# A planner that holds matmuls of another array form back for a while, in a fused attention and two-layer-pair kernel on one core

## The chip, the core and the metric

The kernel runs on one core of a Trainium2 chip. Its engines work side by side, each from its own queue in order: TensorE (PE for matmuls, PEld for the weight loads that precede them), VectorE (DVE), ScalarE (ACT), GpSimd (POOL) and SyncE (SP, which issues nearly all DMAs here). The metric is the device time of one execution in microseconds. Before the change it was 1039.26 us, the median of three runs (1038.78 to 1040.11).

## The reference

Three blocks follow one another. The attention has 4 batches of 8 heads, 576 tokens and 64 columns a head; `f` gives a decay that is added to the scores. Both feed-forward blocks take 2304 tokens of 512 columns through 2048 inner columns.

```
scores = q @ k.T / sqrt(D) + (cum[:, None] - cum[None, :])     # cum = cumsum(log f)
scores = where(causal, -1e9, scores)
attn   = softmax(scores);  x = attn @ v                        # (B, H, S, D) -> (B*S, H*D)
h = x @ w1_in;  g = h * sigmoid(1.702 * h);        x = g @ w1_out
h = x @ w2_in;  g = max(h, 0) + alpha * min(h, 0); out = g @ w2_out
```

All is float32, so most operands are split into a high and a low half, and each product is three matmuls (high by high, high by low, low by high).

## The kernel before

**No hand-written order.** The kernel first describes its work as some thousands of operations (`plan.add`), each with the engines that it may run on, a modelled duration, what it reads and writes, a priority `pri` (a small number goes first) and, for matmuls, a `mode`. Then `Plan.run` (L106) plays all engines through at once: it looks at every operation whose inputs are planned, works out when each could start, takes the one that could start earliest, and among equals the one with the smallest `pri`. What it takes is fixed on its engine at that moment. The list, sorted by planned start, is the program. On the chip every engine goes through its own list in order and waits where something is late; nothing is rearranged there.

**Mode.** TensorE's array can be used in three forms here. Mode 0 is the whole array (128 rows by 128 columns): the turns of q and k (L561), the turn of the maxima (L692), the score products of the last 64 queries (L659, L660), the products of weights and values with split halves (L755), and all products of the feed-forward blocks (L863 for x @ w1_in). Mode 1 uses two halves of 64 rows, one head in each: scores for the maxima (L666), scores for the exponentials (L791), and the product for the 64-row key tile (L732 with a 64-column output). Mode 2 uses two halves of 64 columns (L726, the values of the first 256 queries). The planner adds `SWITCH` = 105 to a matmul operation's modelled end when its mode differs from the one before it (L138); the choice of the next operation (L143, L144) does not look at mode.

**Attention.** Heads go in pairs, queries of a pair in two chunks: 0 to 256 and 256 to 576. That makes 32 chunks; batch 0 has its eight first (four small, four large), then batches 1 to 3 alternate small and large: 12 pairs. A chunk goes through scores for the maximum (L666, L659), masked maximum on DVE (L675), a turn of the maxima (L692) and its eviction (L702), scores again with the maximum as a term (L791), exponentials on ACT (L798), masking on POOL (L714). From chunk 8 on, large chunks split the weights into halves `eh` (a copy on ACT, L370) and `el` (a difference on DVE or POOL, L375), and L755 multiplies `eh` and then `el` by the values. Then DVE normalises (L815 to L832) into the ring `xr`. Two chunks are in work at once.

**Filler.** x @ w1_in (`gemm1`, L842) has seven blocks of 256 or 384 tokens, 16 times 12 matmuls each, 1344 in all. A block may start when the attention has finished its tokens. Its `pri` is 1000 and more, the attention's is 100 to 140, so it fills TensorE wherever no attention operation can start. Its operands `xh` (ACT) and `xl` (DVE) have three and two buffers, so the next block's are made while the last one ends. After the attention, w1_out is converted on ACT and DVE (L501 to L509, L370, L375) while the rest of the filler runs; then come the other three products (L952, L1042, L1120), all in mode 0.

Of the kernel before, what the change touches and what calls it, by code (L numbers as in the profile page):

```python
# [20 lines left out]
BD = 300  # L21
WLAG = 2500.0
SWITCH = 105.0
QUEUE = {"SP": "SP", "ACTQ": "ACT"}


# [46 lines left out]
class Plan:  # L73
# [32 lines left out]
    def run(self):  # L106
        free = {}
        dma = 0.0
        mode = 0
        avail = [o for o in self.ops if o.nd == 0]  # L110
        out = []
        while avail:
            best = None
            for o in avail:
                t0 = o.ready
                need = {}
                for b in o.bufs:
                    t0 = max(t0, b.begin)
                    if b.pool is not None and b.slot is None:
                        p = b.pool  # L120
                        r = p.ready()
                        i = need[p] = need.get(p, -1) + 1
                        if p.nxt + i != b.idx or len(p.free) <= i or p.nxt + i - p.gone >= p.n or r is None:
                            t0 = None
                            break
                        t0 = max(t0, r, p.free[i][0])
                if t0 is None:
                    continue
                alt = None
                for eng, dur, *more in o.alts:  # L130
                    bias, port = (*more, 0.0, False)[:2] if len(more) < 2 else more
                    t = max(t0, free.get(QUEUE.get(eng, eng), 0.0))
                    if port:
                        t = max(t, free.get("port", 0.0))
                    if eng in QUEUE:
                        end = max(t + 1500.0, dma) + dur + 750.0
                    else:
                        end = t + dur + (SWITCH if eng == "PE" and o.mode != mode else 0.0)  # L138
                    key = end + bias
                    if alt is None or key < alt[0]:  # L140
                        alt = (key, t, eng, end, port)
                _, t, eng, end, port = alt
                if best is None or (t, o.pri, end, o.seq) < best[0]:  # L143
                    best = ((t, o.pri, end, o.seq), o, eng, port)  # L144
            assert best is not None, "no operation can start"
            (t, _, end, _), o, eng, port = best
            avail.remove(o)
            o.start, o.eng = t, eng
            if eng == "PE":
                mode = o.mode  # L150
            if eng in QUEUE:
                free[QUEUE[eng]] = t + 480.0
                dma = end - 750.0
            else:
                free[eng] = end
                if port:
                    free["port"] = end
            for b in o.bufs:
                if b.pool is not None and b.slot is None:
                    b.begin, b.slot = b.pool.free.pop(0)  # L160
                    b.begin = max(b.begin, b.pool.ready())
                    b.pool.nxt += 1
            for b in o.bufs:
                b.left -= 1
                b.end = max(b.end, end + LAT)
                if b.left == 0 and b.pool is not None:
                    p = b.pool
                    p.gone += 1
                    p.end = max(p.end, b.end)
                    p.free.append((b.end, b.slot))  # L170
                    p.free.sort()
            for s in o.succ:
                lat = 0.0 if (eng == "PE" and all(a[0] == "PE" for a in s.alts)) else LAT
                s.ready = max(s.ready, end + lat + o.lag)
                s.nd -= 1
                if s.nd == 0:
                    avail.append(s)
            out.append(o)
        assert len(out) == len(self.ops)
        out.sort(key=lambda o: (o.start, o.seq))  # L180
        for o in out:
            o.fn(o.eng)
        return max(o.start for o in out)
# [988 lines left out]
```

## Time and profile before

| | |
|---|---|
| median of the runs | 1039.26 us |
| profiled execution | 1043.87 us, its span 1042.0 us |
| PE / PEld busy | 1012.6 us (97%) / 882.3 us (85%) |
| DVE / ACT / POOL busy | 724.6 (70%) / 514.3 (49%) / 118.1 us (11%) |
| chain that ended last | PE 82%, DMA 7%, DVE 4%, ACT 3%, issue 2% |
| mean granted clock of TensorE | 0.989 of full speed |

The profile shows one execution. "Busy" adds up what an engine's instructions cover; a matmul's end is modelled, and matmuls overlap, so two matmuls' distance from start to start says more about the pace than the duration of one. The chain of waits is followed back from the last instruction to what released it. A row of the timeline joins equal instructions that follow one another; x2 is two of them. Of the two matmuls in a row of L666 or L791, one runs in each half of the array.

### The profile page before, as it was taken

The numbers are of one execution on the slowest core, as the hardware profiler recorded it, in microseconds if no ns is written. First come the engines' busy times: TensorE is split into PE (matmuls) and PEld (weight loads), VectorE is DVE, ScalarE is ACT, GpSimd is POOL, SyncE is SP. The second block draws the span as 40 slices with busy tenths as digits, with TensorE's granted clock in tenths as the row PEclk, the third lists the DMA queues.
The fourth block names the chain that finished last, engine by engine and source line by source line (L and its number), as shares of the span: only waits on it lengthen the run. The fifth ranks groups of instructions, "written<-read, shape, count | busy, mean of one in ns | idle before, by whom it ended". The sixth has DMA issues, their size and how long they took to land.

```text
span 1042.0 us, 17821 instructions
## 1 busy us (share of the span) xinstructions
PE 1012.6 (97%) x6187; PEld 882.3 (85%) x6187; DVE 724.6 (70%) x1528; ACT 514.3 (49%) x1071; POOL 118.1 (11%) x203
## 2 busy tenths in 40 slices
PE   7799999999999999999999999999999999999997
PEld 4477788888888899998888898999999988888886
DVE  5688887777766692109998565676994876676773
ACT  4367654453444483228776464455863742222322
POOL 5133422211221000000000000000300110000000
PEclk8899999999999999999999999999999999999999
DMA  4577744323311195225667354465775443443441
GB/s 104 120 195 185 186 111 89 73 66 76 76 52 44 47 295 179 102 92 163 220 193 228 100 148 141 166 196 167 221 268 176 156 128 115 118 142 84 126 140 65
DMA packets 180089, 144.69 MB, mean 139 GB/s; under 512 B 101152, under 2 KB 155088, under 8 KB 180000
## 3 DMA queue, kind: packets, MB, share of 16 engines
q1 hardware_dynamic: 180000, 143.57, 47.0%
q8 instruction: 48, 0.79, 0.3%
q14 instruction: 41, 0.34, 0.1%
HBM read 96.14 MB, written 47.33 MB: 138 GB/s over the span
## 4 chain that ended last, share of the span: by engine, by line
PE 82%; DMA 7%; DVE 4%; ACT 3%; issue 2%; SPq 1%; POOL 1%; ACTq 0%; DVEq 0%; POOLq 0%
PE bk L1120 19%; PE bk L863 17%; PE bk L952 17%; PE bk L1042 11%; PE bk L791 5%; PE bk L755 4%; DMA wraw<-in_moe_w_out_dram 3%; PE bk L726 3%; PE bk L666 2%; PE bk L732 2%; DMA h2scr<-go 1%; DMA wraw<-in_moe_w_in_dram 1%; DMA rk<-in_k_dram 1%; PE bk L659 1%; DVE wraw L506 1%
## 5 line engine op out<-in xcount | busy, mean ns | idle before, releaser
L863 PE MATMUL bk<-xh,wA 128*128 128x384 f32 (+1 forms) x896 | 224.1, 321 | 0.0
L370 ACT CAST qh<-qg 128x512 fp32r<-128x512 f32 (+1 forms) x159 | 91.9, 579 | 171.6 <-DVE qg L918 118.0
L375 DVE TENSOR_TENSOR ql<-qg,qh 128x512 fp32r<-128x512 f32 (+1 forms) x158 | 100.5, 637 | 101.4 <-PE bk L952 49.5
L863 PEld LDWEIGHTS bk<-xh,wA 128*128 128x128 f32 x896 | 158.6, 190 | 12.2 <-issue 8.5
L1120 PE MATMUL bk<-wS,qh 128*128 128x512 f32 x576 | 145.7, 389 | 0.0
L863 PE MATMUL bk<-xl,wA 128*128 128x384 f32 (+1 forms) x448 | 140.7, 314 | 0.6 <-DVE xl L375 0.6
L1120 PEld LDWEIGHTS bk<-wS,qh 128*128 128x128 f32 x576 | 108.1, 188 | 22.4
L1042 PE MATMUL bk<-xsb,wS 128*128 128x384 f32 x576 | 108.9, 336 | 3.2 <-DVE go L1064 2.7
L370 ACT COPY gg<-bk 128x384 f32<-128x384 f32 (+1 forms) x112 | 48.7, 435 | 122.1 <-PE bk L863 119.3
L1042 PEld LDWEIGHTS bk<-xsb,wS 128*128 128x128 f32 x576 | 100.2, 188 | 6.0 <-DVE go L1064 4.4
L675 DVE CUSTOM_DVE_ANT_0 bk<-bk,mask 128x512 f32<-128x512 f32 (+4 forms) x160 | 75.3, 496 | 38.6 <-PE bk L666 35.3
L952 PE MATMUL bk<-qh,woa 128*128 128x512 f32 (+1 forms) x440 | 99.5, 368 | 0.1
L952 PEld LDWEIGHTS bk<-qh,woa 128*128 128x128 f32 x440 | 77.3, 189 | 14.2 <-ACT qh L370 0.5
L863 PEld LDWEIGHTS bk<-xl,wA 128*128 128x128 f32 x448 | 85.2, 190 | 1.2 <-DVE xl L375 1.0
L798 ACT ACTIVATE e<-bk 128x384 f32<-128x384 f32 (+3 forms) x192 | 59.5, 400 | 51.0 <-PE bk L791 46.0
L1042 PE MATMUL bk<-xsa,wS 128*128 128x384 f32 x432 | 82.5, 334 | 0.0
L1120 PE MATMUL bk<-wS,ql 128*128 128x512 f32 x288 | 80.4, 389 | 0.0
L1042 PEld LDWEIGHTS bk<-xsa,wS 128*128 128x128 f32 x432 | 75.6, 188 | 0.2
L911 DVE SCALAR_TENSOR_TENSOR qg<-qg,qr 128x512 f32<-128x512 f32 (+1 forms) x80 | 50.8, 636 | 24.6 <-ACT qg L910 24.4
L1120 PEld LDWEIGHTS bk<-wS,ql 128*128 128x128 f32 x288 | 54.0, 188 | 11.2
L910 ACT ACTIVATE qg<-qr 128x512 f32<-128x512 f32 (+1 forms) x80 | 46.9, 588 | 22.0 <-DVE ql L375 18.9
L952 PE MATMUL bk<-ql,woa 128*128 128x512 f32 (+1 forms) x220 | 54.1, 368 | 0.0
(161 smaller groups left out, 1748.0 us busy)
## 6 DMA issues: line engine op xcount, KB each, us to landing
h2scr<-go SPq DMA_DIRECT2D x96, 192.0 KB
wraw<-in_moe_w_in_dram SPq DMA_DIRECT2D x32, 512.0 KB
wraw<-in_moe_w_out_dram SPq DMA_DIRECT2D x32, 512.0 KB
qr<-h1scr SPq DMA_DIRECT2D x64, 256.0 KB
qr<-h2scr SPq DMA_DIRECT2D x64, 256.0 KB
h1scr<-gg SPq DMA_DIRECT2D x64, 192.0 KB
ba<-y1scr SPq DMA_DIRECT2D x24, 384.0 KB
h1scr<-gg SPq DMA_DIRECT2D x48, 128.0 KB
```

The source lines that it names most:

```text
L370: nc.scalar.copy(dst, src)
L375: E[e].tensor_tensor(dst, a, b, op=ALU.subtract)
L675: plan.add([("DVE", c_dve(c1 - c0) + 90.0)], lambda e, pm=pm, c0=c0, c1=c1, mk=mk, m0=m0, col=col, f0=f0: nc.vector.tensor_tensor_reduce(p ...
L755: nc.tensor.matmul(pb[hh].ap[:l.shape[1], s0 - q0:n], l, rhs.ap[:w, hh, :m], start=st, stop=sp, skip_group_check=True,)
L791: nc.tensor.matmul(pss[hh].ap[:w, o_:o_ + m], x.ap[r, a:a + w], y.ap[r, s0 - q0:n], start=i == 0, stop=i == 3, skip_group_check=True)
L798: plan.add([("ACT", c_act(x1 - x0, True))], lambda e, hh=hh, pss=pss, e32=e32, w=w, x0=x0, x1=x1: nc.scalar.activation(e32.ap[:w, hh, :x1 ...
L863: nc.tensor.matmul(ph.ap[:, :n], w.ap[:, a, c, :], x[c // 2].ap[:, c % 2, :n], start=(c == 0 and j == 0), stop=(c == KT - 1 and j == 2))
L910: plan.add([("ACT", c_act(n))], lambda e: nc.scalar.activation(g.ap[:, :n], raw.ap[:, :n], AF.Tanh, scale=0.851), [raw], [g], pri)
L911: plan.add([("DVE", c_dve(n), 0.0, True)], lambda e: nc.vector.scalar_tensor_tensor(g.ap[:, :n], g.ap[:, :n], 1.0, raw.ap[:, :n], op0=ALU. ...
L952: nc.tensor.matmul(py[d].ap[:, :n], w[:, a, d * P:(d + 1) * P], (lo if x else h).ap[:, :n], start=(k == 0 and (a, x) == (0, 0)), stop=(k = ...
L1042: nc.tensor.matmul(out.ap[:, :XH], w[:, a, t, c, :], x.ap[:, b, c, :], start=(st and c == 0 and i == 0), stop=(c == 1 and i == 2), skip_gr ...
L1120: nc.tensor.matmul(py[t].ap, (lo if x else h).ap[:, t * P:(t + 1) * P], w[:, a], start=(k == 0 and (a, x) == (0, 0)), stop=(k == NM - 1 an ...
```

## The change

Two constants are added, and the planner's choice is altered. A TensorE operation whose mode is not the current one, and whose inputs and buffers have been there for less than 2000 ns of planned time, is ranked as if it started 250 ns later; its planned start, once it is taken, stays the true one. So as long as an operation of the current form can start within 250 ns, it goes first, whatever the priorities; after 2000 ns the rank is the old one. Nothing is computed in another way: the program has the same 4173 rows of TensorE instructions, in another order.

```
+PEN = 250.0
+HOLD = 2000.0
...
                 _, t, eng, end, port = alt
-                if best is None or (t, o.pri, end, o.seq) < best[0]:
-                    best = ((t, o.pri, end, o.seq), o, eng, port)
+                hold = PEN if eng == "PE" and o.mode != mode and t - t0 < HOLD else 0.0
+                if best is None or (t + hold, o.pri, end, o.seq) < best[0]:
+                    best = ((t + hold, o.pri, end, o.seq), o, eng, port, t)
             assert best is not None, "no operation can start"
-            (t, _, end, _), o, eng, port = best
+            (_, _, end, _), o, eng, port, t = best
```

Because of the added lines, a line from L150 on has a number that is 3 higher in the changed kernel (L863 is L866 there).

**TensorE, a middle pair of chunks.** Names: `bk` is a PSUM bank, `KH`, `QH`, `QL`, `KL` are halves of k and q, `DK`, `DQ` hold decay and maximum, `eh`, `el` halves of the weights, `VH`, `VL`, `VR` the values, `xh`, `xl`, `wA` operands of the filler. Before, scores of a new small chunk stand between products with values, and the first maximum scores of a large chunk follow alone, with filler behind them:

```order
L791 MATMUL bk_88<-DQ_100,DK_95 128x256
L791 MATMUL bk_84<-DQ_100,DK_95 128x256
L755 MATMUL bk_86<-eh_1600,VH_107 128x320
L755 MATMUL bk_81<-eh_1600,VH_107 128x320
L755 MATMUL bk_86<-eh_1600,VL_109 64x320
L755 MATMUL bk_81<-eh_1600,VL_109 128x320
L755 MATMUL bk_86<-el_1630,VH_107 128x320
L755 MATMUL bk_81<-el_1630,VH_107 128x320
L666 MATMUL bk_85<-KH_174,QH_258 128x384
L666 MATMUL bk_83<-KH_174,QH_258 128x384
L666 MATMUL bk_85<-DK_95,ones 128x384
L666 MATMUL bk_83<-DK_95,ones 128x384
```

With the change, the maximum scores of the large chunk, the waiting 64-row product (L735) and the small chunk's scores stand in one run:

```order
L669 MATMUL bk_86<-KH_230,QH_233 128x384
L669 MATMUL bk_82<-KH_230,QH_233 128x384
L669 MATMUL bk_86<-DK_96,ones 128x384
L669 MATMUL bk_82<-DK_96,ones 128x384
L735 MATMUL bk_88<-e_377,VR_104 128x64
L735 MATMUL bk_85<-e_377,VR_104 128x64
L794 MATMUL bk_84<-QH_177,KH_230 128x128
L794 MATMUL bk_81<-QH_177,KH_230 128x128
L794 MATMUL bk_84<-QL_184,KH_230 128x128
L794 MATMUL bk_81<-QL_184,KH_230 128x128
L794 MATMUL bk_84<-QH_177,KL_236 128x128
L794 MATMUL bk_81<-QH_177,KL_236 128x128
```

The twelve rows before hold two changes of form (at the first L755 and the first L666), and filler follows as a third; the twelve rows after hold none. Counted by form over the whole program, with L726 as a form of its own, there are 232 changes before and 153 after. Up to the 224th matmul of L791, which ends the first eight chunks, it is 50 and 42; behind it, 182 and 111. A middle pair of chunks goes from 16 to 18 changes to 8.

**DVE, the `el` halves of the same kind of chunk.** Before, the first two `el` of a large chunk follow two copies of the next q and k and stand together:

```order
L372 CAST QH_233<-tq_837 128x256
L372 CAST KH_230<-tk_856 128x576
L375 TENSOR_TENSOR el_1630<-e_456,eh_1600 128x640
L375 TENSOR_TENSOR el_1619<-e_384,eh_1594 128x640
L375 TENSOR_TENSOR QL_240<-tq_837,QH_233 128x256
L375 TENSOR_TENSOR KL_236<-tk_856,KH_230 128x576
L540 STREAM_TRANSPOSE tq_837<-rq_130 128x320
```

With the change, a small chunk's normalisation (reciprocal, L825, L835) and a q half stand around and between them:

```order
L824 RECIPROCAL rc_399<-sm_392 128x8
L378 TENSOR_TENSOR el_1556<-e_532,eh_1533 128x640
L825 STREAM_TRANSPOSE tr_385<-rc_399 128x256
L378 TENSOR_TENSOR QL_240<-tq_789,QH_233 128x256
L835 TENSOR_TENSOR xr<-bk_83,tr_385 128x256
L378 TENSOR_TENSOR el_1540<-e_377,eh_1523 128x640
```

What stands ahead of the second `el` behind the first is now three instructions more.

**ACT, the end of the attention.** `wc`, `wraw` are weights being converted, `qh` an operand of L952, `gg` an evicted filler product. Before, the copies `xh` of a filler block come late in the conversion of w1_out:

```order
L501 ACTIVATE wc_518<-wraw_405 128x512
L370 COPY gg_722<-bk_84 128x384
L502 ACTIVATE wraw_405<-wraw_405 128x512
L501 ACTIVATE wc_499<-wraw_412 128x512
L370 COPY gg_815<-bk_88 128x384
L502 ACTIVATE wraw_412<-wraw_412 128x512
L370 COPY gg_680<-bk_83 128x384
L370 CAST xh_1095<-xr 128x768
L370 COPY gg_722<-bk_82 128x384
L370 CAST xh_473<-xr 128x768
```

With the change they stand in the middle of it, since the filler is further on:

```order
L504 ACTIVATE wc_515<-wraw_425 128x512
L373 CAST qh_4630<-qg_4561 128x512
L505 ACTIVATE wraw_425<-wraw_425 128x512
L373 CAST qh_4642<-qg_4537 128x512
L373 COPY gg_694<-bk_87 128x384
L373 CAST woa_4655<-wc_554 128x512
L373 CAST xh_1100<-xr 128x768
L373 COPY gg_787<-bk_88 128x384
L373 CAST xh_490<-xr 128x768
```

When the attention's last product is issued, 750 filler matmuls have been issued before and 852 after. From there to the first L952 it is 210 of them before and 108 after; from that L952 on, TensorE's order is the same in both.

## Rows read from the trace of the kernel before

**Rows 1.** Six stretches, TensorE first: busy us and instructions per engine, clock, DMA share, GB/s.

```profile
0.00:107.00 107.00, 89.24 (x661) 66.31 (x662) 77.13 (x221) 59.42 (x145) 38.36 (x82) 0.92 0.63 152
107.00:358.00 251.00, 248.75 (x2100) 209.05 (x2099) 188.54 (x528) 115.89 (x306) 57.01 (x106) 0.99 0.34 81
358.00:465.00 107.00, 106.37 (x610) 105.51 (x610) 38.91 (x66) 48.96 (x95) 0.00 (x0) 1.00 0.49 164
465.00:660.00 195.00, 194.88 (x951) 164.97 (x950) 150.96 (x268) 126.84 (x226) 0.00 (x0) 1.00 0.53 164
660.00:838.00 178.00, 174.76 (x995) 171.92 (x994) 132.81 (x207) 107.74 (x205) 16.75 (x11) 1.00 0.61 200
838.00:1042.00 204.00, 198.62 (x880) 164.52 (x878) 136.28 (x240) 55.45 (x97) 5.98 (x4) 0.99 0.38 112
```

**Rows 2.** What TensorE waited for: us in total, times, longest us.

```profile
PE bk L666 <- DMA DK<-xr: 4.9, 2, 4.4
PE bk L1042 <- DVE go L1064: 2.7, 3, 1.3
PE bk L666 <- ACT e L798: 2.2, 1, 2.2
```

**Rows 3.** Timeline of TensorE in a middle pair: start us, us, instruction.

```profile
228.08 0.31 PE L791 MATMUL bk<-DQ,DK 64*128 64x320 f32 x2
...
229.13 0.39 PE L863 MATMUL bk<-xh,wA 128*128 128x256 f32 x1
...
230.04 0.41 PE L791 MATMUL bk<-QH,KH 64*128 64x320 f32 x2
230.28 0.31 PE L791 MATMUL bk<-QL,KH 64*128 64x320 f32 x2
...
230.58 0.31 PE L791 MATMUL bk<-DQ,DK 64*128 64x320 f32 x2
230.82 0.34 PE L692 MATMUL bk<-ident_r,MX 128*67 128x128 f32 x2
...
233.03 0.56 PE L755 MATMUL bk<-el,VH 128*128 128x320 f32 x2
...
238.49 0.41 PE L863 MATMUL bk<-xh,wA 128*128 128x256 f32 x2
...
238.84 0.40 PE L863 MATMUL bk<-xh,wA 128*128 128x256 f32 x2
...
244.49 0.66 PE L726 MATMUL bk<-e,VR 128*64 128x128 f32 x8
```

**Rows 4.** The same pair on ScalarE, timeline.

```profile
228.42 2.05 ACT L798 ACTIVATE e<-bk 128x320 f32<-128x320 f32 x8 [1.30 <-PE bk L791]
230.34 1.37 ACT L370 CAST eh<-e 128x640 fp32r<-128x640 f32 x2
```

**Rows 5.** The same pair on VectorE, timeline.

```profile
231.37 1.55 DVE L375 TENSOR_TENSOR el<-e,eh 128x640 fp32r<-128x640 f32 x2
```

**Rows 6.** ScalarE behind the attention, timeline.

```profile
362.86 1.14 ACT L370 CAST woa<-wc 128x512 fp32r<-128x512 f32 x2
...
377.49 0.63 ACT L370 CAST woa<-wc 128x512 fp32r<-128x512 f32 x1
```

**Rows 7.** VectorE at the end of a filler block, timeline.

```profile
396.64 1.82 DVE L375 TENSOR_TENSOR xl<-xr,xh 128x768 fp32r<-128x768 f32 x2
```

**Rows 8.** TensorE at the same place, timeline.

```profile
394.83 2.01 PE L952 MATMUL bk<-qh,woa 128*128 128x512 f32 x8
...
397.65 0.45 PE L863 MATMUL bk<-xl,wA 128*128 128x384 f32 x1 [0.63 <-DVE xl L375]
```

**Rows 9.** SyncE near the start, timeline of DMA issues.

```profile
32.62 5.19 SPq L612 DMA_DIRECT2D VR<-in_v_dram  x2
```

**Rows 10.** TensorE near the start, timeline.

```profile
41.18 0.69 PE L666 MATMUL bk<-DK,ones 64*128 64x384 f32 x2 [4.37 <-DMA DK<-xr]
```

**Rows 11.** A short stretch by itself, columns as in rows 1.

```profile
118.00:122.00 4.00, 4.00 (x20) 2.64 (x20) 3.70 (x11) 1.24 (x5) 2.43 (x3) 0.57 0.69 215
```

## The prediction

> **What bounds the kernel now.** I read the stretches first, then what TensorE waited for, then the timeline of one pair of chunks on three engines. In the stretch from 107 to 358 us, where the attention of batches 1 to 3 runs among the filler, matmuls cover 248.75 of 251 us; to 107 us they cover only 89.24, and behind 358 us nearly everything [rows 1]. The waits of TensorE are few: 4.9 us for the DMA of the decay near the start, 2.2 us for exponentials, 2.7 us in the third product [rows 2]. ACT and DVE have 115.89 and 188.54 busy us in the 251 us of the middle stretch [rows 1], so TensorE's own work is what sets the time there, and whatever is taken out of its list comes out of the end, unless something else becomes late.
>
> Busy is not the same as fast, though, and the timeline shows where. Steady filler of 256 columns goes from start to start in (238.84 - 238.49) / 3 = 0.117 us. A lone run of six, between two runs of 64-row scores, takes from 229.13 to 230.04, 0.91 us, where six steady ones take 0.70: 0.21 us too much. A lone run of eight 64-row score matmuls takes from 230.04 to 230.82, 0.78 us, where four steady pairs of 0.15 us (230.28 to 230.58 for two) take 0.60: 0.18 us too much [rows 3]. Each run pays once, so a change of form costs between 0.18 and 0.21 us. I take 0.19.
>
> The Trainium skill ("Trainium Kernel Development and Optimization", Performance Expectations) says that busy time of matmuls is a poor measure of how near TensorE is to its limit and that the busy share of weight loads is a better one. By matmul time the middle stretch has 2.25 us to give; by weight loads it would have 251 - 209.05 = 42 us, which the sum below does not use.
>
> **The change part by part.** *Changes of form.* From the order there are 232 before and 153 after. The first eight chunks account for 50 and 42, what follows for 182 and 111. The 71 that go in the later part are in the stretch where TensorE does not wait [rows 1]: 71 x 0.19 = 13.5 us. By the two ends of the cost it is 71 x 0.18 = 12.8 to 71 x 0.21 = 14.9 us.
>
> *The first eight chunks.* Eight changes go, worth at most 8 x 0.21 = 1.7 us, but TensorE stands still here for 107 - 89.24 = 17.8 us anyway [rows 1], so most of that is cover lost elsewhere. The largest single wait is 4.37 us for the decay [rows 10]. Its DMA is queued on SP behind the load of a V tile, whose two issues took 5.19 us [rows 9]. With the change one large weight load stands behind these rather than ahead of them, and three of the four decay loads stand ahead of the V tile; the fourth is still behind it, and the products need all four. So between 4.4 us less and, if another wait of that size arises from the new order, 4.4 us more. I take 0, the middle, since nothing else in the rows leans either way.
>
> *Waits inside the attention.* Where scores run in succession, products follow sooner upon them. In a middle pair with the change, from the last score matmuls of the first 320-wide key tile to its product with `el`, TensorE has one pair (0.15), the small chunk's second product (0.5, from its 0.66 us with the overlapping end), three changes (0.57), two pairs of 256-wide maximum scores (0.23), eight pairs of scores (1.2), six filler matmuls (0.70) and four products (four of 0.15, as 320 columns take for a pair, 0.6): 3.9 us [rows 3]. The same path by ACT and DVE: exponentials start 0.34 us behind that score row (228.42 - 228.08), four of 0.26 are 1.0, one `eh` 0.69 and one `el` 0.78, 2.8 us together [rows 3, 4, 5]. But before the change the first `el` was done only at 231.37 + 0.78 = 232.15, 4.1 us behind the scores, since eight exponentials and both `eh` went first; it was used at 233.03 [rows 3, 5]. So the wait is between 0 and 0.2 us. The second `el` has, by the same pieces, some 3.65 us from its scores (one pair, eight scores, one change, six filler, ten products of 0.15, 0.5 for the 192-wide one), and took 232.92 - 228.67 = 4.25 us before (228.67 is four pairs behind 228.08) [rows 3, 5]; three more DVE instructions now stand ahead of it, and fewer exponentials. Less the 0.2 us already waited, that is 0 to 0.4 us. For a pair 0 to 0.6 us; the exponentials ahead are halved, so I take 0.15, nearer to the lower end. Twelve pairs: 1.8 us, bounds 0 and 7.2.
>
> The other side of holding back, that the filler might run out, does not come about: with the change, 852 of 1344 filler matmuls are issued when the attention ends, against 750, and 960 may be issued by then (five blocks of 192).
>
> *The end of the attention.* Only 108 filler matmuls stand between the attention and the first L952 now, 210 before. At 106.37 / 610 = 0.174 us each [rows 1] they cover 18.8 us, and the eight L952 about 1.8 more. By then the next block's `xh` and `xl` must be there. On ACT the first weight copy started 4.9 us behind the attention's end on TensorE (362.86 against the border at 358), and 27 instructions went by from 362.86 to 377.49, 0.54 us each [rows 6]; `xh` now has 28 ahead of it, so it starts at about 4.9 + 15.2 = 20.1 us, and with 0.9 for it and 0.9 for `xl` [rows 7] the operand is there at 21.9, needed at 20.6. That is a wait of 1.3 us where before there was 0.63 [rows 8]: 0.7 us more. It would be 0 if ACT goes faster, and 2 if the second `xh` is late too. Everything from there on has the same order on TensorE and starts as much earlier as the attention ends.
>
> *The sum.* 13.5 - 0 - 1.8 - 0.7 = 11.0 us. The profiled execution took 1043.87 us (span 1042.0), so it would take 1032.9; the median of the runs, 1039.26, lies 4.6 us below the profiled one, and from it the same subtraction gives 1028.3. I predict 1028.
>
> **Rivals.** *The softmax side sets the pace.* The bursts of scores come faster than ACT and DVE can follow, at both `el`. For it speak the 4.1 and 4.25 us that the paths took before; against it, that DVE is busy for only 188.54 of 251 us and that `eh` no longer stands behind eight exponentials [rows 1, 4, 5]. At the upper bound, 0.6 us a pair, it is 7.2 us in place of 1.8: 1028.3 + 5.4 = 1033.7. The Trainium skill ("TensorEngine Tiling (Array Packing)", Performance Considerations, PSUM Bottleneck) says that using the array in tiles speeds up TensorE but not the emptying of PSUM, which may then be the limit; by that rule this rival is the case.
>
> *The same, so far that it turns the sign.* The place is the two products with `el` in each of the twelve pairs. It decides from 13.5 / 12 = 1.1 us of waiting a pair. If each of the two products comes 1.0 us too early, as when the second group of exponentials (four of 0.26) goes ahead of `eh` on ACT after all, and the second `el` then loses nothing of the first one's wait, a pair loses 2.0 us, 24 us in all: 1039.3 - 13.5 + 24 + 0.7 = 1050.5; at 1.5 us a pair it would be 1044.5. Against it: the first wait also delays the second use, and by the pieces above the first `el` has 3.9 us for a path of 2.8.
>
> *The start decides.* The order of its loads and first chunks changes most for its length. Without the 4.37 us wait: 1024; with another one: 1032. A long wait costs more than itself: behind the 2.2 us wait for exponentials at 116 us the granted clock was 0.57 of full speed from 118 to 122 us [rows 2, 11], that is mostly the lower level of 1.2 GHz, and some 1.7 us of work were lost. Such a wait more is 4 us, one less gives 4 us back.
>
> *The cost lies elsewhere.* If half of the 0.19 us belongs to the run's first semaphore wait and not to the form, the gain is 6.7 - 2.5 = 4.2 us: 1035. Against it: the change from L791 to L692 at 230.82, which is a turn of maxima and no filler, pays as the filler does [rows 3].
>
> **How the numbers follow.** A difference of 0.2%, 2.1 us, is about what a measurement can tell from none. The forecast, 1023 to 1032.5 with the start's smaller shifts: 0.69. Better than that through the start: 0.06. The softmax side at its pace or half of the cost, 1032.5 to 1037.2: 0.14. Within 0.2%: 0.05. Slower: 0.06. So faster 0.89, same 0.05, slower 0.06. The range 1021.5 to 1035 leaves out a part of the third case and the last two, and little below.
>
> **What would show it.** In the profile with the change: the runs of L863 and L791 between changes longer, and each still some 0.2 us over the steady pace; weight loads at a larger share than 209.05 of 251 us in the middle; the attention's last product some 4 us later than 358 us, since 102 more filler matmuls (102 x 0.15 = 15 us at a mean of both widths) stand ahead of it, less 11; the first L952 about 11 us earlier than 394.83. Wrong would be: waits of L755 for `el` (DVE or POOL) over 0.3 us in most pairs, a wait over 2 us at the first block border behind the attention, or a start that is more than 4 us off.

## The result, and the profile after

The changed kernel takes 1022.84 us (median of 6 runs, 1020.42 to 1024.27); the kernel before took 1039.68 us beside it (6 runs, 1038.78 to 1041.75). The ratio is 0.9834, 95% interval 0.9819 to 0.9849: 16.8 us faster. The forecast was 1028.0 in a range of 1021.5 to 1035, so the sign and the range held and the gain is 5.2 us larger than forecast.

The profiled execution took 1022.32 us (span 1020.6), close to its median. The profiled execution of before took 1043.87, which is 4.2 us above the median of its runs. The two profiles therefore differ by 21.5 us, 4.7 more than the medians, and a part of the waits in the earlier trace is not typical of that kernel. Where sizes matter below, medians decide.

From the profile page after the change: the busy times, and the chain that ended last.

```profile
PE 995.1 (98%) x6187; PEld 880.2 (86%) x6187; DVE 711.2 (70%) x1506; ACT 522.1 (51%) x1087; POOL 125.7 (12%) x209
...
PE 89%; DMA 4%; DVE 3%; issue 1%; ACT 1%; SPq 1%; POOL 0%; DVEq 0%; ACTq 0%; POOLq 0%
```

The chain was 82% PE and 7% DMA before. The first five of the six stretches, the borders put at the same places of the program (busy us and instructions of PE, PEld, DVE, ACT, POOL, then clock, DMA share, GB/s):

```profile
0.00:100.00 100.00, 86.76 (x659) 65.73 (x660) 71.99 (x213) 57.76 (x142) 36.05 (x81) 0.93 0.68 156
100.00:356.00 256.00, 252.78 (x2205) 225.20 (x2204) 182.69 (x518) 130.79 (x336) 66.94 (x113) 1.00 0.36 89
356.00:375.00 19.00, 19.00 (x112) 19.00 (x111) 17.85 (x34) 16.15 (x32) 0.00 (x0) 1.00 0.73 238
375.00:639.00 264.00, 263.99 (x1345) 233.61 (x1344) 169.57 (x299) 154.02 (x280) 0.00 (x0) 1.00 0.52 164
639.00:817.00 178.00, 174.11 (x996) 172.28 (x996) 132.88 (x208) 108.06 (x205) 16.72 (x11) 1.00 0.61 198
```

Against [rows 1], the share of weight loads in the attention's stretch rises from 209.05 of 251 us (83%) to 225.20 of 256 (88%), as expected if TensorE pauses less between matmuls (it does 105 more of them in this stretch), and matmuls cover 252.78 of 256. The stage of L955 is again full; the third product (639 to 817) is as long as it was.

What TensorE waited for (us in total, times, longest):

```profile
PE bk L564 <- DMA rk<-in_k_dram: 9.0, 4, 4.0
PE bk L1045 <- DVE go L1067: 3.9, 4, 1.9
...
PE bk L669 <- DMA DK<-xr: 1.4, 1, 1.4
...
PE bk L758 <- ACT eh L373: 0.2, 1, 0.2
```

The wait for the decay fell from 4.9 to 1.4 us and the one for exponentials (L666 on ACT `e`, 2.2 us) is gone [rows 2]; `eh` costs 0.2 us in all. The load of k (`rk`) is waited for longer. It was already the largest sum before, which [rows 2] leave out:

```profile
PE bk L561 <- DMA rk<-in_k_dram: 6.4, 3, 4.1
```

The timeline of a middle pair of chunks on TensorE, the place of [rows 3]:

```profile
230.72 0.31 PE L794 MATMUL bk<-DQ,DK 64*128 64x320 f32 x2
...
231.55 0.39 PE L669 MATMUL bk<-KH,QH 64*128 64x256 f32 x2
...
232.32 0.30 PE L794 MATMUL bk<-DQ,DK 64*128 64x320 f32 x2
232.47 0.31 PE L794 MATMUL bk<-QH,KH 64*128 64x320 f32 x2
...
232.90 0.31 PE L794 MATMUL bk<-DQ,DK 64*128 64x320 f32 x2
233.14 0.39 PE L866 MATMUL bk<-xh,wA 128*128 128x256 f32 x1
233.37 0.28 PE L866 MATMUL bk<-xl,wA 128*128 128x256 f32 x1
233.48 0.40 PE L866 MATMUL bk<-xh,wA 128*128 128x256 f32 x2
...
233.96 0.47 PE L758 MATMUL bk<-eh,VH 128*128 128x320 f32 x2
...
234.56 0.45 PE L758 MATMUL bk<-el,VH 128*128 128x320 f32 x2
...
236.08 0.46 PE L758 MATMUL bk<-el,VH 128*128 128x320 f32 x2
```

One run of 64-row scores now goes from 231.55 to 233.14, and each of its rows (a pair) starts some 0.145 us behind the last (232.32 to 232.47). The last pair, 232.90, is followed 0.24 us later by the filler: 0.095 too much. The filler's first matmul, 233.14, is followed 0.23 us later by its second, where 0.117 is the steady pace: 0.11 too much. So a change of form has two halves, one ahead of it and one behind its first matmul, 0.2 us together.

The halves `eh` on ScalarE and `el` on VectorE of that pair:

```profile
231.06 1.21 ACT L801 ACTIVATE e<-bk 128x320 f32<-128x320 f32 x4 [1.30 <-PE bk L794]
232.31 0.73 ACT L373 CAST eh<-e 128x640 fp32r<-128x640 f32 x1
...
234.09 0.74 ACT L373 CAST eh<-e 128x640 fp32r<-128x640 f32 x1
```

```profile
233.07 0.83 DVE L378 TENSOR_TENSOR el<-e,eh 128x640 fp32r<-128x640 f32 x1
...
234.91 0.81 DVE L378 TENSOR_TENSOR el<-e,eh 128x640 fp32r<-128x640 f32 x1
```

The scores of the first key tile end with the row at 230.72. Four exponentials, one `eh` and one `el` (each 0.7 to 0.8 us) follow, and that `el` is done at 233.07 + 0.83 = 233.90, 3.2 us behind the scores; it was 4.1 us before, when eight exponentials and both `eh` went first [rows 4, 5]. It is used at 234.56. The second key tile's scores end with the row at 232.32, its `el` is done at 235.72, 3.4 us later, and used at 236.08. Neither product waits.

The start, TensorE at the decay and at the load of k:

```profile
29.20 0.33 PE L669 MATMUL bk<-DK,ones 64*128 64x128 f32 x2 [1.37 <-DMA DK<-xr]
...
45.61 0.96 PE L564 MATMUL bk<-ident,rk 128*128 128x128 f32 x3 [3.55 <-DMA rk<-in_k_dram]
```

The 4.37 us wait for the decay at 41.18 [rows 10] is gone, and a 3.55 us wait for k stands four microseconds later: one wait for a load was traded for another. The end of the attention, TensorE at the first border between filler blocks:

```profile
374.75 0.33 PE L866 MATMUL bk<-xh,wA 128*128 128x384 f32 x1
374.93 2.01 PE L955 MATMUL bk<-qh,woa 128*128 128x512 f32 x8
376.78 0.34 PE L866 MATMUL bk<-xh,wA 128*128 128x384 f32 x1
```

The first L955 starts at 374.93 in place of 394.83 [rows 8], and the filler behind its eight follows without the 0.63 us wait.

**A budget.** If I take the time to the first product of the second stage (L952, L955), and subtract every idle stretch of TensorE over 20 ns and the time lost at a reduced clock while it worked, what is left is the pace of the list itself. Before: 394.8 - 20.0 - 8.9 = 366.0 us. After: 374.9 - 16.5 - 6.5 = 352.0. The same first part ran five times more in the experiments below and gave 351.5 to 352.1, so for one order this number repeats to some 0.3 us. The list got 14.0 us shorter by 79 changes of form less: 0.177 us each. What this budget can't see is a short wait: a matmul of 256 columns is drawn 0.28 us long where the next one starts after 0.117, so TensorE may stand still for some 0.16 us without a gap, and such waits stay in the list.

### The profile page after: what moved, and what is told of

It is laid out like the page before. It is cut to its first block, busy times and chain, and to the rows that moved or that the text cites. A ratio compares the mean times of both kernels' runs of the same rounds, so it can differ in the third digit from the quotient of the medians.

```text
span 1020.6 us, 17794 instructions
## 1 busy us (share of the span) xinstructions
PE 995.1 (98%) x6187; PEld 880.2 (86%) x6187; DVE 711.2 (70%) x1506; ACT 522.1 (51%) x1087; POOL 125.7 (12%) x209
## 4 chain that ended last, share of the span: by engine, by line
PE 89%; DMA 4%; DVE 3%; issue 1%; ACT 1%; SPq 1%; POOL 0%; DVEq 0%; ACTq 0%; POOLq 0%
PE bk L866 20%; PE bk L955 19%; PE bk L1123 19%; PE bk L1045 13%; PE bk L794 5%; PE bk L758 3%; PE bk L669 2%; PE bk L735 2%; PE bk L729 2%; DMA rk<-in_k_dram 1%; DMA h2scr<-go 1%; DMA ba<-y1scr 1%; PE bk L695 1%; PE bk L564 1%; DMA wraw<-in_moe_w_out_dram 1%
## 5 line engine op out<-in xcount | busy, mean ns | idle before, releaser
L866 PE MATMUL bk<-xh,wA 128*128 128x384 f32 (+1 forms) x896 | 220.0, 319 | 1.5 <-POOL wA L378 1.3
L866 PEld LDWEIGHTS bk<-xh,wA 128*128 128x128 f32 x896 | 156.4, 189 | 12.3 <-issue 5.8
L866 PE MATMUL bk<-xl,wA 128*128 128x384 f32 (+1 forms) x448 | 140.0, 312 | 0.0
L955 PE MATMUL bk<-qh,woa 128*128 128x512 f32 (+1 forms) x440 | 99.5, 368 | 0.0
L955 PEld LDWEIGHTS bk<-qh,woa 128*128 128x128 f32 x440 | 77.3, 189 | 14.0 <-ACT qh L373 0.4
L866 PEld LDWEIGHTS bk<-xl,wA 128*128 128x128 f32 x448 | 84.6, 189 | 0.1
L955 PE MATMUL bk<-ql,woa 128*128 128x512 f32 (+1 forms) x220 | 54.1, 368 | 0.0
```

The lines of the kernel that those rows point to most:

```text
L866: nc.tensor.matmul(ph.ap[:, :n], w.ap[:, a, c, :], x[c // 2].ap[:, c % 2, :n], start=(c == 0 and j == 0), stop=(c == KT - 1 and j == 2))
L955: nc.tensor.matmul(py[d].ap[:, :n], w[:, a, d * P:(d + 1) * P], (lo if x else h).ap[:, :n], start=(k == 0 and (a, x) == (0, 0)), stop=(k = ...
```

## Experiments

In every run below the time of the kernel before, beside it on the same chip, was 1039.1 to 1039.7 us, and ratios are to that.

**Which part of the program gains.** The hold only ahead of 100 us of planned time (e1), and only behind it (e2):

```
# e1
hold = PEN if eng == "PE" and o.mode != mode and t - t0 < HOLD and t < 100000.0 else 0.0
# e2
hold = PEN if eng == "PE" and o.mode != mode and t - t0 < HOLD and t > 100000.0 else 0.0
```

> The changed kernel, with the hold only for operations that the planner would start before its 100 us; behind that the old rule. 224 changes of form in all, 42 up to the end of the first eight chunks and 182 behind it, against 42 and 111 in the full change and 50 and 182 before. Theory (a removed change of form gives 0.19 us in the middle, and the first eight chunks give something of their own): the gain of the start alone, which the profiles of before and after put at 5.3 us, less what lies in their run-to-run difference: 1034 to 1038 us. Rival (all of the gain is the count of changes, 0.19 us each, wherever they stand): 8 fewer, 1.5 us, 1038 us. Rival (the start is only luck of one execution): 1039.5 us.

> The changed kernel, with the hold only for operations that the planner would start after its 100 us. 170 changes of form, 50 up to the end of the first eight chunks as before and 120 behind it (182 before, 111 with the full change). Theory (0.195 us a change in the middle, worked out from both profiles): 62 x 0.195 = 12.1 us off 1039.7, and 0.6 us from the wait at the first block border behind the attention: 1027 us; the first 105 us of the profile as before. Rival (the gain comes from the start, whose waits for DMAs are shorter with the full change): 1035 us or more.

Measured: e1 1036.16 us (1034.98 to 1037.65, ratio 0.9965, 0.9951 to 0.9978), 3.5 us faster than before. e2 1026.61 us (1026.18 to 1030.72, ratio 0.9883, 0.9864 to 0.9902), 13.0 us faster. Together 16.5, so the two parts add up to the whole change (16.8) well within their intervals. The later part is the forecast's main term, 62 changes less in this order. In e2 192 filler matmuls more stand ahead of the first L955; with 0.174 us each taken off for them, its list is 352.4 us, so the budget gives 366.0 - 352.4 = 13.6 us, 0.22 us each; e1's eight changes are 366.0 - 364.4 = 1.6 us, 0.2 each. The budgets don't add up change by change, though: 70 changes give 15.2 us here, the 79 of the whole change 14.0. In the attention a change is thus priced to between 0.18 and 0.22 us and no closer.

The other half of e1's 3.5 us is then not the changes. The runs point to the clock: over the whole execution TensorE was granted 0.992 to 0.995 of full speed in the five runs of e1, 0.983 to 0.989 in the nine of the kernel before beside it, and 0.986 to 0.991 in the five of e2, which keeps the old start. Between the two traces, TensorE lost 8.9 us at a reduced clock while it worked before and 6.2 us in e1. Which wait lowers the clock is not settled: the 2.2 us wait for exponentials, behind which it fell [rows 2, 11], is in none of the traces taken later, and there is one trace of the kernel before.

**What one change costs, outside the attention.** The changed kernel with one short extra matmul ahead of each of the 72 products of the third stage that start a fresh bank, with no form change (e3, all 128 rows) and with two (e4, 64 rows); what they add is overwritten by the product.

```
+            if st:
+                nc.tensor.matmul(
+                    out.ap[:, :64], w[0:64, 0, t, 0, :], x.ap[0:64, 0, 0, 0:64],   # e4; e3: 0:128
+                    start=True, stop=True, skip_group_check=True,
+                )
```

> The changed kernel with 72 small matmuls more (128 rows, 128 x 64, into a bank that the next matmul overwrites) ahead of the first, fifth and sixth product of every pair in the third product's stage, which is all in mode 0. No change of form. Every theory: 72 times a short matmul with its weight load, 0.06 to 0.1 us, so 4 to 7 us more than 1022.8: 1027 to 1030 us.

> As the kernel with 72 small matmuls of 128 rows, but these have 64 rows: 144 changes of form more, in a stage without attention. Theory (each change of form costs 0.19 to 0.2 us by itself): 144 x 0.195 = 28 us over the kernel with 128 rows, 1055 to 1058 us. Rival (half of the excess of a run belongs to waits of the attention's operations and not to the form): 14 us over it. Rival (nothing of it is the form): the same time as with 128 rows.

Measured: e3 1028.94 us (1028.79 to 1029.33, ratio 0.9894, 0.9881 to 0.9908); e4 1050.09 us (1049.61 to 1050.57, ratio 1.0097, 1.0083 to 1.0111). The difference, 21.15 us over 144 changes, is 0.147 us each, three quarters of what was expected. Form alone costs time, since the two kernels differ in nothing else, but less than the attention shows. TensorE around one extra matmul, e3 and then e4:

```profile
699.81 0.19 PE L1044 MATMUL bk<-xsa,wS 128*128 128x64 f32 x1
699.84 1.28 PE L1050 MATMUL bk<-xsa,wS 128*128 128x384 f32 x6
```

```profile
702.17 0.29 PE L1044 MATMUL bk<-xsa,wS 64*128 64x64 f32 x1
702.40 1.31 PE L1050 MATMUL bk<-xsa,wS 128*128 128x384 f32 x6
```

In e3 the short matmul is followed 0.03 us later by the next, which then pays for the weights that could not be loaded behind it: 253 ns to its successor in place of 174 (medians of 72). In e4 the medians are 268 ns from the last full matmul to the short one (174 steady), 223 to the next (30 steady), and 279 to the one behind (174): 393 ns over the steady pace, 0.197 for each of two changes. Less the 80 ns that e3 pays anyway it is 0.157, near what was measured. So a run of one short matmul is a poor gauge, and the next pair repeats it with three matmuls of 384 columns:

```
+                for i in range(3):
+                    nc.tensor.matmul(
+                        out.ap[:, :XH], w[0:64, i % 2, t, i // 2, :], x.ap[0:64, 0, 0, :],   # e6; e5: 0:128
+                        start=(i == 0), stop=(i == 2), skip_group_check=True,
+                    )
```

> The changed kernel with three extra matmuls of 384 columns on all 128 rows ahead of each of the 72 products of the third stage that start a fresh bank; no change of form is added (what they add up is overwritten, since the product starts its bank anew). All theories: 72 x 3 x 0.174 = 37.6 us over the changed kernel, about 1060.5. It is the base for the next run.

> The same three extra matmuls on 64 rows, so that each run of three is one to another form and one back: 144 changes more. Theory A, a change costs about 0.195 us wherever the run on each side is long enough to show both halves (0.09 before it and 0.105 behind it), and the lone short matmul before gave only 0.147 because its own short length left no steady second matmul: 144 x 0.195 = 28 us over the base, about 1088.5. Theory B, a change in the array itself costs 0.147 us and the rest of the 0.195 seen in the attention belongs to something else there (a semaphore wait at the head of each run): 144 x 0.147 = 21 us over the base, about 1081.7.

Measured: e5 1055.41 us (1054.32 to 1057.15, ratio 1.0162, 1.0147 to 1.0177), e6 1086.44 us (1084.65 to 1087.45, ratio 1.0456, 1.0442 to 1.0469). The difference, 31.0 us over 144, is 0.215 us a change. Theory A holds: the whole cost shows where runs are long enough. (The base came 5 us below what was expected. Part of it is that the three matmuls fill TensorE's waits for `go`, 3.9 us in the changed kernel's trace and 1.9 in that of its repeat, e11; e5 has none. The rest is not explained.) TensorE around one run of three, matmuls and weight loads, e5 and then e6:

```profile
701.81 0.68 PE L1045 MATMUL bk<-xsa,wS 128*128 128x384 f32 x3
702.33 1.20 PE L1051 MATMUL bk<-xsa,wS 128*128 128x384 f32 x6
```

```profile
701.64 0.54 PEld L1045 LDWEIGHTS bk<-xsa,wS 128*128 128x128 f32 x3
```

```profile
700.72 1.20 PE L1051 MATMUL bk<-xsb,wS 128*128 128x384 f32 x6
701.85 0.79 PE L1045 MATMUL bk<-xsa,wS 64*128 64x384 f32 x3
702.57 2.36 PE L1051 MATMUL bk<-xsa,wS 128*128 128x384 f32 x12
```

```profile
701.85 0.47 PEld L1045 LDWEIGHTS bk<-xsa,wS 64*128 64x128 f32 x3 [0.25 <-issue]
702.57 1.17 PEld L1051 LDWEIGHTS bk<-xsa,wS 128*128 128x128 f32 x7 [0.25 <-issue]
```

In e5 the run of three takes 702.33 - 701.81 = 0.52 us, 0.173 each; in e6 702.57 - 701.85 = 0.72. From start to start (medians of 72) e6 has 268 ns from the last 128-row matmul to the run, 281 from its first to its second, then 175, 265 out of it, 281, and 177; e5 has 173 or 174 everywhere. That is 403 ns over for two changes, 0.20 us each. The weight loads tell why: in e5 the load for the run starts at 701.64, 0.17 us ahead of its matmul; in e6 it starts with its matmul, at 701.85, behind 0.25 us without a load. The next load then starts late as well, 0.107 us behind the run's first matmul in place of 0.003 (medians), and that is the second half. The Trainium skill ("TensorEngine Tiling (Array Packing)", Tiling Modes, Key Properties) says that changing the tiling mode drains TensorE. The trace agrees in that the loads pause for 0.25 us at each change; it costs the two halves above, 0.2 us together.

**More of the same.** A handicap of 1000 ns in place of 250 (e7), and the hold for 4000 ns in place of 2000 (e8):

```
# e7
-PEN = 250.0
+PEN = 1000.0
# e8
-HOLD = 2000.0
+HOLD = 4000.0
```

> The changed kernel with a handicap of 1000 ns in place of 250. By the order 29 changes in the first eight chunks in place of 42, and 106 behind them in place of 111. Theory A, every change costs 0.195 us also near the start: 18 x 0.195 = 3.5 us less, 1019.3. Theory B, in the start TensorE waits anyway, so only the 5 later ones count: 1.0 us less, 1021.8. Rival C, a long handicap makes TensorE stand still or delays the chain of the chunks (maxima, exponentials) so that filler must wait later: slower than the changed kernel, 1024 to 1030.

> The changed kernel with the handicap kept for 4000 ns in place of 2000. By the order 34 changes in the first eight chunks in place of 42, and 107 in place of 111 behind them. Theory A, every change costs 0.195 us also near the start: 12 x 0.195 = 2.3 us less, 1020.5. Theory B, only the later 4 count: 0.8 us less, 1022.0. Rival C, the longer hold delays the chunks: 1024 to 1030.

Measured: e7 1031.99 us (1030.69 to 1033.11, ratio 0.9933, 0.9921 to 0.9945); e8 1038.81 us (1035.72 to 1044.64, ratio 0.9998, 0.998 to 1.0016). Both lose against the changed kernel, 9 and 16 us, with 18 and 12 changes fewer: theory C in both, beyond its price. Four stretches of e7, and then one of the changed kernel:

```profile
0.00:34.00 34.00, 23.97 (x165) 16.59 (x165) 20.05 (x73) 16.71 (x36) 15.17 (x50) 0.84 0.50 129
34.00:62.00 28.00, 20.89 (x120) 15.18 (x120) 17.41 (x48) 10.30 (x21) 6.65 (x7) 0.62 0.64 156
...
95.00:113.00 18.00, 14.99 (x120) 12.64 (x119) 15.31 (x38) 11.42 (x29) 6.84 (x7) 1.00 0.84 215
113.00:387.00 274.00, 272.49 (x2322) 244.59 (x2319) 193.01 (x537) 139.96 (x353) 65.91 (x114) 1.00 0.35 89
```

```profile
34.00:52.00 18.00, 14.04 (x114) 11.12 (x115) 12.90 (x39) 8.09 (x21) 3.30 (x6) 0.79 0.61 157
```

From 113 us on, e7 is as good as its count promises (its list is 349.8 us in the budget, the shortest of all). The loss lies in the first chunks. They end at 113.0 us in place of 98.6 (98.6 to 102.2 in the six traces that have the changed kernel's order there and behind it). TensorE covers only 20.89 of the 28 us from 34 to 62, and the granted clock there is 0.62, mostly the lower level of 1.2 GHz, where the changed kernel has 0.79 from 34 to 52. Idle time of the first chunks is 20.7 us against 13.2 to 16.8 in those six, and the clock takes 14.8 us in place of 5.5 to 7.1. In e8 most of the loss lies in the attention, where TensorE is idle for 9.3 us against 2.6 to 3.2. What TensorE waited for in the whole program, then its timeline near the attention's end, and beside it VectorE and ScalarE (the profiled execution, 1036.09 us, is one of its faster ones):

```profile
PE bk L695 <- DVE MX L678: 5.4, 6, 2.5
...
PE bk L695 <- POOL MX L687: 3.5, 3, 2.0
```

```profile
375.06 0.34 PE L866 MATMUL bk<-xh,wA 128*128 128x384 f32 x1
...
377.50 0.27 PE L695 MATMUL bk<-ident_r,MX 128*67 128x128 f32 x1
380.27 0.28 PE L695 MATMUL bk<-ident_r,MX 128*67 128x128 f32 x1 [2.50 <-DVE MX L678]
...
385.82 0.56 PE L758 MATMUL bk<-eh,VH 128*128 128x320 f32 x2 [0.59 <-ACT eh L373]
...
389.98 0.34 PE L866 MATMUL bk<-xh,wA 128*128 128x384 f32 x1
```

```profile
386.54 0.42 DVE L835 TENSOR_TENSOR xr<-bk,tr 128x256 f32<-128x256 f32 x1
```

```profile
387.37 1.57 ACT L373 CAST xh<-xr 128x768 fp32r<-128x768 f32 x2
```

Between 375.06 and 389.98 no filler matmul is issued, 14.9 us. With nothing to put in between, TensorE stands 2.50 us for a maximum, turns it, issues the scores, and waits again for `eh`. There are such stretches without filler at 178.7 and 291.6 us too (14.8 and 19.1 us); the longest behind the first chunks in the changed kernel is under 8. Why no filler comes can be read from the last two rows. Each of the three stretches begins when twelve matmuls of a new block have been issued; its other ones need the block's next `xh`, and that copy starts only when the attention has written its last tokens of the block into `xr` (386.54, then `xh` at 387.37, then filler at 389.98). So the filler has run out because the attention itself is late. The attention's last product comes at 391.2 us, with 978 filler matmuls issued by then, 852 in the changed kernel.

**Is there a better dose?** The start as in the changed kernel, and only behind 100 us of planned time a hold of 2500 (e9) or 3000 ns (e10), with the changed kernel itself once more beside them (e11):

```
hold = PEN if eng == "PE" and o.mode != mode and t - t0 < (HOLD if t < 100000.0 else 2500.0) else 0.0   # e10: 3000.0
```

> The changed kernel, with the hold 2500 ns in place of 2000 only behind 100 us of planned time; the first eight chunks are as in the changed kernel. By the order 107 changes of form behind them in place of 111, and 876 filler matmuls issued when the attention ends in place of 852 (the last blocks of the filler are free only then). Theory A, the time goes with the number of changes: 4 x 0.195 = 0.8 us less than the changed kernel, about 1022. Theory B, what decides is whether filler is left to cover the chain of scores, maxima and turn: it is still left here, so also about 1022.

> The same with 3000 ns behind 100 us of planned time. By the order only 101 changes there in place of 111, but 1008 filler matmuls issued when the attention ends in place of 852, against 978 with 4000 ns everywhere, which lost 16 us. Theory A, the time goes with the number of changes: 10 x 0.195 = 2.0 us less than the changed kernel, about 1021. Theory B, the filler runs out before the attention ends, TensorE then waits for the maxima with nothing to put in between, and the attention's last product comes at 380 us or later in place of 356: 6 to 16 us more than the changed kernel, 1029 to 1039.

> The changed kernel itself once more, beside the two others on the same chip, so that their small differences are read against it: 1022.8 by all theories.

Measured: e9 1025.72 us (1022.9 to 1027.87, ratio 0.9862, 0.9839 to 0.9884), e10 1024.84 (1023.09 to 1025.21, ratio 0.9853, 0.9839 to 0.9866), e11 1023.5 (1022.73 to 1025.5, ratio 0.9846, 0.9832 to 0.986). The three can't be told apart, and no run beat the change. Neither theory holds for e10: the 10 changes less brought nothing that the runs show, and 1008 filler matmuls issued at the attention's end cost nothing either, since its trace has no stretch over 8 us without filler behind the first chunks (it stops after the same twelve matmuls at 368.12, for 7.3 us, with 0.2 us of idle time). It is thus not how much filler has gone by the end that decides, but whether some is free at each place where the chain of scores, maxima and turn is short of cover. By the budget, with the 192 filler matmuls taken off in e10 as in e2, e9 and e10 come to 352.1 and 352.5 us, no less than the changed kernel's 351.5 to 352.1; where the 0.8 and 2.0 us of the changes went was not settled.

## Why the prediction was right, and where its sizes were off

- **TensorE's own list sets the time, and a change of form costs 0.18 to 0.21 us: right.** 13.5 us was forecast for the 71 later changes. By e2 the later part gives 13.0 us (10.2 to 14.1 by its interval) with 62 changes less; in the changed kernel the whole list is 14.0 us shorter with 79 less; and e6 measures 0.20 to 0.215 us for a change with no attention around it. The rival that half of it is a semaphore wait falls with e6.
- **The first eight chunks: mis-sized.** The step took 0, "the middle, since nothing else in the rows leans either way". e1 measured -3.5 us (-2.3 to -5.1 by its interval). 1.6 us of it are the eight changes, which the step had valued at "at most 1.7" and then set to nothing because TensorE stands still there anyway. That is the error: only 17.8 of 105 us are idle, and between the waits the list has its pace here too. The rest goes with a higher granted clock, 0.993 against 0.988 in the medians of the runs; the sum has no term for it, though the rival on the start names it. On the loads the zero came out by luck: the 4.37 us wait for the decay was traded for 3.55 us at k, a load that the step doesn't name. The prediction's list of TensorE's waits leaves out the largest sum, 6.4 us for k in three waits, which became 9.0 in four.
- **Waits for `el`, 1.8 us: too high.** No product waits for `el`; 0.2 us for one `eh` is all. TensorE reaches the two products 3.84 and 3.76 us behind their scores, as the step had it (3.9 and 3.65). But it carried the second path over from before at 4.25 us, and with fewer exponentials ahead it takes 3.4; the three DVE instructions that were to delay it fit into the time in which it waits for its `eh`. So the softmax side at its pace, and the same with the sign turned, both fall here. The point from which a wait decides does exist, and e8 found it elsewhere, at the turn of the maxima when no filler is free.
- **The tail, 0.7 us of waiting: too high.** There is no wait at the border; the 0.63 us of before went too.
- **The sum.** Forecast 13.5 - 0 - 1.8 - 0.7 = 11.0; measured 13.0 + 3.5 = 16.5 by the two parts, `el` and tail being within the later one. The three smaller terms all erred to the same side, so nothing cancelled. Of the signs that were named, two were off: the attention's last product was to be some 4 us later than 358 and is at 356.0 (358.4 in e11), and the first product of the second stage came 19.9 us earlier (17.6 in e11) in place of about 11, because the start and the waits gave their share ahead of them.

## What to carry to other kernels

Count changes of array form in a list that TensorE is never idle in, and price one from the trace as the excess of the last matmul before it plus the excess of the first behind it; here about 0.2 us. Grouping pays until what is held back is the chain that feeds the next work, or the cover runs out: past that point, here with a hold of 4000 ns, 12 changes less came with 16 us more. A term in a stretch with waits is not zero: only the idle share of it is cover.

## What was not expected of the hardware

- A change of form is paid in two halves, 0.095 us between the last matmul of one form and the first of the next, and 0.107 us between that one and its second, because the first weight load of the new form doesn't run ahead (at 701.85 with its matmul, against 0.17 us ahead in the run without change), and the second starts 0.107 us behind that matmul. A run of a single short matmul pays only 0.147 us a change, since a load that could not hide behind so short a matmul is paid with and without the change.
- The clock moves with the waits near the start, and it can weigh more than they do. In e7 it was 0.62 of full speed over 28 us; up to the second stage it cost 14.8 us against 6.5 in the changed kernel, while the idle time grew from 13.2 to 20.7. In e1, with less idle time in its trace (16.2 us against 17.8 before), every run was granted a higher clock than any run of the kernel before beside it.
